# Ten of ten rows per gather and float32r scores in a talking-heads attention followed by two feed-forward stages

## The chip, the cores and the metric

One NeuronCore of a Trainium2 chip runs the whole program. The metric is the device time of one execution in microseconds. TensorE (PE in the profile; PEld is its weight load) multiplies, VectorE (DVE), ScalarE (ACT) and GpSimd (POOL) do the element-wise work, and SyncE's queue (SPq) issues the data transfers.

## The reference, cut to what matters

There are 4 batches, 12 heads, 448 positions and a head width of 64. Scores are mixed across the heads before the softmax (`w_pre`) and the probabilities are mixed across the heads after it (`w_post`). Two feed-forward stages on 1792 tokens of width 768 follow.

```python
scores = scale * np.matmul(q, k.transpose(0, 1, 3, 2))
scores = np.einsum('bhij,hg->bgij', scores, w_pre)
attn = softmax(scores)                       # over the last axis
attn = np.einsum('bhij,hg->bgij', attn, w_post)
x = (attn @ v), heads side by side           # 1792 x 768
h = x @ w_in;  x = (h * clip(h + 3, 0, 6) / 6) @ w_out     # 768 -> 2048 -> 768
return ((x @ w1) * (x @ w2)) @ w3 @ w_out2   # 768 -> 1024 -> 1024 -> 768
```

The feed-forward weights arrive as 64-bit floats; the kernel unpacks them itself. q, k and v are float32.

## The kernel before

**Attention.** The 448 query rows of a batch are cut into four chunks (`ci`, 16 in all). For a chunk, `load_q` (line 344) loads q, and for every first chunk of a batch `load_k` (line 353) loads k in three pieces. `scores` (line 366) is called six times per chunk, each time for two heads, 96 times in all: one head has its 64 contraction rows in partitions 0 to 63, the other in 64 to 127. Each is one float32 matmul of 64 rows by 110 or 120 query columns against 448 keys, into a PSUM bank of its own. The trace shows a float32 matmul as two instructions, so a call has four. `out` (line 387) copies the two heads to the tile `s`, whose partitions are queries, by ScalarE or VectorE.

**The mix.** `mix` (line 392) handles one slot: two groups of nine query rows of one batch. There are 25 slots per batch, 100 in all. Each group is fetched by `gather` (line 403), a transfer that turns ten partitions of `s` (nine query rows of this group and one that belongs to another) times twelve heads into 120 partitions of the tile `g`: rows 0 to 59 carry five query rows with their twelve heads, rows 60 to 119 the other five. `premix` (line 411) multiplies by block weights in four quarters of the array (4 matmuls, 8 instructions), `rowmax` (line 419, VectorE) takes the maximum, `softexp` (line 424, ScalarE, two halves) the exponentials and their sums, `guard` (line 431, GpSimd as a rule) adds 1e-9, `recip` and `weigh` (lines 436 and 441, VectorE) make weights of the reciprocal, and `postmix` (line 455) multiplies by them in 32 small float32 matmuls (64 instructions). `evac` (line 469) copies the result out of PSUM in two parts. After the slots of half a batch, `values` (line 479) multiplies by v, six calls per half batch, 48 in all, and the result goes to DRAM through the tile `x`.

**Feed-forward.** Line 598 on: `Line.weight` loads each block of weights, unpacks it on ScalarE and VectorE, and splits it into a high and a low float32r part; `product` (line 679) then makes three float32r products (high x high, high x low, low x high). `up` (line 688) and `down` (line 708) are its users.

**The order of the work** is written by a planner before the program starts. `Plan.add` (line 99) takes the engine or the choice of engines, an estimated duration and a priority; `Plan.run` (line 135) plays the program through with those estimates and fixes for each engine the order in which it runs its instructions. On the chip each engine follows that order, and an instruction that waits holds up everything behind it on its engine. `URGE` (line 69) holds offsets of the priorities and the slot pace, `unit0`, 3.845. For work that can go to several engines the first named is preferred; another takes it if the preferred one is planned busy for more than a set number of nanoseconds (`pGuard`, 226.69, for the guard). `SHARED` (line 72) says which tiles live in which buffers; `BUFS` (line 262) how many there are: 4 of `g`, 5 of `k`, 3 of `q`, 4 of `x`, and 4 pairs of PSUM banks shared by all matmuls. The first feed-forward weights may start to load when the last q load (`gate["q"]`, line 349) has been issued and landed.

The lines that later steps rest on:

```python
GROUP = 9
GROUPS = [12, 12, 13, 13]
BLOCKS = G0[4] // 2
...
mm(p.t[:M, i, :S], q.t[d, hp * M:(hp + 1) * M], k.t[d, hp % 2], True, True)
op = plan.add("PE", 950, prio, emit, read=(q, k), ...
...
nc.sync.dma_start(out=g.t[:120, y], in_=st.t[p0:p0 + 9 * d + 1:d])
...
plan.add({"Pool": 250, "DVE": 140}, 0, at + URGE["norm"], guard, use=(z,), wait="Guard")
```

## Time and profile before

| what | value |
|---|---|
| three runs, us | 1309.34, 1313.62, 1320.05 (median 1313.62) |
| profiled execution: span from first to last instruction, us | 1319.0 |
| profiled execution: own time | no other figure than the span is listed; of the three runs the highest, 1320.05, lies nearest, 1.05 above it |
| TensorE busy | 1270.9 us, 96% |
| VectorE busy | 924.2 us, 70% |
| ScalarE busy | 490.4 us, 37% |
| GpSimd busy | 344.8 us, 26% |
| mean granted TensorE clock | 0.991 |

A busy time is the sum of an engine's instructions, not a share of its peak. Instructions of TensorE overlap, so the step from the start of one operation to the start of the next tells more than the duration of one. The line number of every matmul is 237, that of the helper which issues it; the tile names (`sc`, `pre`, `post`, `val`, `up`, `dn`) tell them apart.

### The profile page before, as it was taken

Reading aid. Unit: us, or ns where it says so; the run is one execution under the profiler, and the core shown is the slowest. Engines: PE = TensorE matmul, PEld = TensorE weight load, DVE = VectorE, ACT = ScalarE, POOL = GpSimd, SP = SyncE. Lnnn points to the kernel's source line nnn. Section 1 sums busy time; section 2 is a strip of 40 time slices with the busy share of each in tenths; the row PEclk is TensorE's granted clock in tenths of the full one; section 3 lists DMA queues with packets and bytes.
Section 4 is the critical chain, followed back from the end, with each engine's and each line's share of the span. In section 5 each row is a group of like instructions: output and inputs, shape, how many; then the busy total and the mean of one; then the engine's idle time right before and its main releaser. Section 6 shows DMA issues by size and latency. Waiting matters only on the chain.

```text
span 1319.0 us, 30151 instructions
## 1 busy us (share of the span) xinstructions
PE 1270.9 (96%) x12768; PEld 1033.1 (78%) x12768; DVE 924.2 (70%) x1424; ACT 490.4 (37%) x972; POOL 344.8 (26%) x311
## 2 busy tenths in 40 slices
PE   7899999999989999999999999999999999999998
PEld 3446555555568899889898989998989999999997
DVE  2667766757697789989989988966357556654533
ACT  5656655556575442232322232333134111111110
POOL 0000000000034344443234333334443222322211
PEclk9999999999999999999999999999999999999999
DMA  5766746646664334323232233314443111211003
GB/s 150 205 180 157 239 144 173 209 131 177 190 210 140 132 108 135 116 86 93 91 96 88 88 112 104 95 52 139 151 144 100 37 39 46 60 37 36 12 28 140
DMA packets 75574, 154.06 MB, mean 117 GB/s; under 512 B 7152, under 2 KB 42672, under 8 KB 75440
## 3 DMA queue, kind: packets, MB, share of 16 engines
q1 hardware_dynamic: 75440, 152.14, 38.2%
q8 instruction: 100, 1.64, 0.5%
q14 instruction: 34, 0.28, 0.1%
HBM read 88.32 MB, written 20.78 MB: 83 GB/s over the span
## 4 chain that ended last, share of the span: by engine, by line
PE 44%; DVE 12%; DMA 4%; issue 3%; POOL 1%; ACT 1%; POOLq 0%; SPq 0%; DVEq 0%
PE up L237 24%; PE dn L237 16%; PE w L237 5%; DVE raw L637 2%; DMA raw<-w_in 2%; DVE raw L641 2%; DVE raw L639 2%; DVE raw L633 1%; DVE acc L729 1%; DVE raw L631 1%; DVE w L644 1%; DMA w3dram<-raw 1%; ACT raw L624 1%; POOL raw L644 1%; DMA raw<-w_out 1%
## 5 line engine op out<-in xcount | busy, mean ns | idle before, releaser
L237 PE MATMUL up<-act,w 128*128 128x448 f32 x2160 | 458.9, 366 | 0.0
L237 PEld LDWEIGHTS up<-act,w 128*128 128x128 f32 x2160 | 404.7, 188 | 37.1
L237 PE MATMUL dn<-gs,w 128*128 128x448 f32 x1728 | 376.2, 369 | 10.4 <-POOL gs L240 7.3
L237 PEld LDWEIGHTS dn<-gs,w 128*128 128x128 f32 x1728 | 324.6, 189 | 44.4 <-POOL gs L240 10.8
L729 DVE TENSOR_TENSOR acc<-acc,dn 128x896 f32<-128x896 f32 x168 | 181.4, 1081 | 79.1 <-PE dn L237 77.5
L240 POOL TENSOR_TENSOR w<-raw,w 128x768 fp32r<-128x768 f32 (+1 forms) x65 | 126.8, 1952 | 206.7 <-ACT w L312 129.0
L240 POOL TENSOR_TENSOR gs<-t,gs 128x448 fp32r<-128x448 f32 (+1 forms) x58 | 95.2, 1642 | 300.8 <-ACT gs L312 290.9
L237 PEld LDWEIGHTS post<-wt,e 60*64 60x64 f32 (+1 forms) x6400 | 111.4, 137 | 63.3 <-issue 42.7
L624 ACT ACTIVATE raw<-raw 128x384 f32<-128x384 f32 (+1 forms) x136 | 71.5, 528 | 234.5 <-DMA raw<-w 68.2
L427 ACT ACTIVATE e<-pre,m 128x448 f32<-128x448 f32 x200 | 125.9, 637 | 36.9 <-DVE m L421 30.4
L421 DVE TENSOR_REDUCE m<-pre 128x2 f32<-128x896 f32 x100 | 107.6, 1086 | 42.4 <-PE pre L237 41.7
L237 PE MATMUL post<-wt,e 60*64 60x60 f32 (+1 forms) x6400 | 118.5, 222 | 17.2 <-issue 12.6
L312 ACT CAST gs<-t 128x448 fp32r<-128x448 f32 (+1 forms) x60 | 45.0, 750 | 192.1 <-DVE t L885 124.4
L432 POOL TENSOR_SCALAR z<-z 128x2 f32<-128x2 f32 x97 | 21.9, 226 | 353.3 <-ACT e L427 349.9
L237 PE MATMUL pre<-g,wih 56*64 56x448 f32 (+1 forms) x800 | 104.8, 561 | 8.6 <-DMA g<-s 6.8
L237 PE MATMUL sc<-k,q 64*120 64x448 f32 (+1 forms) x384 | 93.6, 588 | 5.0 <-DMA k<-kd 5.0
L631 DVE TENSOR_SCALAR raw<-raw 128x768 f32<-128x768 f32 (+1 forms) x68 | 61.6, 907 | 42.8 <-ACT raw L624 39.6
L637 DVE SCALAR_TENSOR_TENSOR raw<-raw 128x384 int32<-128x384 int32 (+1 forms) x136 | 79.5, 623 | 1.6
L641 DVE SCALAR_TENSOR_TENSOR raw<-raw 128x384 f32<-128x384 uint32 (+1 forms) x136 | 79.2, 608 | 0.3
L312 ACT CAST w<-raw 128x768 fp32r<-128x768 f32 (+1 forms) x55 | 43.6, 793 | 79.8 <-PE w L237 30.2
L237 PE MATMUL w<-w 128*128 128x512 f32 (+1 forms) x384 | 68.6, 337 | 0.0
L237 PEld LDWEIGHTS pre<-g,wih 60*64 60x64 f32 (+1 forms) x800 | 24.9, 133 | 55.7 <-issue 15.7
(69 smaller groups left out, 1114.6 us busy)
## 6 DMA issues: line engine op xcount, KB each, us to landing
g<-s SPq DMA_DIRECT2D x200, 210.0 KB
raw<-w SPq DMA_DIRECT2D x48, 384.0 KB
raw<-w_in SPq DMA_DIRECT2D x28, 384.0 KB
raw<-w_out SPq DMA_DIRECT2D x28, 384.0 KB
raw<-w3t SPq DMA_DIRECT2D x32, 256.0 KB
v<-vd SPq DMA_DIRECT2D x12, 512.0 KB
raw<-w4dram SPq DMA_DIRECT2D x16, 384.0 KB
k<-kd SPq DMA_DIRECT2D x12, 448.0 KB
```

Of the source, the lines that this page charges most:

```text
L237: nc.tensor.matmul(o, lhsT=lt, rhs=rh, start=start, stop=stop)
L240: eng.tensor_tensor(out=o, in0=a, in1=b, op=ALU.subtract)
L312: nc.scalar.copy(o, i)
L421: nc.vector.tensor_reduce(out=m.t, in_=pre.t[:, :, :S], axis=AX.X, op=ALU.max, negate=True)
L427: nc.scalar.activation(out=e.t[:, a_], in_=pre.t[:, a_, :S], func=ACTF.Exp, bias=m.t[:, a_:a_ + 1], accum_out=z.t[:, a_:a_ + 1])
L624: nc.scalar.mul(value()[:, halves[i]], f(bits(i))[:, :, 1], 2.0 ** -112)
L631: one(out=f(y), in0=f(y), scalar1=F64_TOP, scalar2=-F64_TOP, op0=ALU.min, op1=ALU.max)
L637: two(out=y, in0=hi, scalar=-0x80000000, in1=y, op0=ALU.bitwise_and, op1=ALU.bitwise_or)
L639: one(out=hi, in0=y, scalar1=-0x800000, scalar2=None, op0=ALU.bitwise_and)
L641: two(out=f(hi), in0=lo, scalar=2.0 ** -52, in1=f(hi), op0=ALU.mult, op1=ALU.mult)
L644: (nc.gpsimd if e == "Pool" else nc.vector).tensor_tensor(out=o[:, halves[i]], in0=x[:, halves[i]], in1=f(bits(i))[:, :, 1], op=ALU.add)
L729: nc.vector.tensor_tensor(out=o(), in0=o(), in1=p.t[:, :, :S], op=ALU.add)
```

## The change

A group is now ten query rows, all ten that a gather fetches, and a slot is twenty: 23 slots per batch, the last of which holds one group (8 of whose ten rows exist), 92 slots and 180 gathers in all (200 before). The gather lands at partitions 4 to 123 of `g`, so that the two sets of five rows lie in partitions 4 to 63 and 64 to 123; partitions 0 to 3 are set to zero by a new GpSimd memset (`blank`) that each slot's gathers wait for. Chunks become 120, 120, 110 and 98 query rows.

The scores become three float32r products per head (high x high, high x low, low x high), six matmuls per call in place of two float32 ones. For them a new function `halve` splits each load of q and of k into a high and a low part: q in two pieces (six for the first chunk), k in two. The high part is a copy, on GpSimd, or on ScalarE or VectorE if GpSimd is planned busy for over 123 ns; the low part is a subtraction, on GpSimd or VectorE. Raw loads of both share the three `q` buffers, the k halves have six `k` buffers, the q halves four new `u` buffers; `w` goes from 5 to 1 (with `u` added to its places) and `x` from 4 to 2. The scratch space of dynamic transfers is set to 1024, and offsets in `URGE` change with the pace left at 3.845.

```diff
 
 SET = 5
 ROWS = 12 * SET
-GROUP = 9
-GROUPS = [12, 12, 13, 13]
-APART = [g - 1 for g in GROUPS]
+GROUP = 2 * SET
+BEFORE = 64 - ROWS
+GROUPS = [12, 12, 11, 10]
 G0 = [sum(GROUPS[:c]) for c in range(5)]
-BLOCKS = G0[4] // 2
...
 LEN = [GROUP * g for g in GROUPS[:3]]
 LEN.append(S - sum(LEN))
-WIDE = [10 * d for d in APART]
+WIDE = [GROUP * d for d in GROUPS]
...
-            first, d = group_rows(c, t)
-            G = G0[c] + t
-            for i, r in enumerate((0, 1, 2, 3, 4, 6, 7, 8, 9)[:GROUP - (G >= G0[4] - 2)]):
-                order[WD0[c] + first + d * r] = GROUP * G - (G == G0[4] - 1) + i
+            for r in range(GROUP):
+                row = GROUP * (G0[c] + t) + r
+                if row < S:
+                    order[WD0[c] + t + GROUPS[c] * r] = row
...
 SHARED = dict(
-    accs=("pth",), acts=("ptl",), gs=("e", "g"), t=("e", "g"), act0=("s",), act3=("s",),
-    w=("k", "w"), raw=("q", "raw"), early=("w0", "w1", "w2", "k"), first=("q", "r0", "r1", "r2", "raw"), stg=("x",), stage=("raw", "w"),
+    accs=("pth",), acts=("ptl",), kraw=("q",), qraw=("q",), khl=("k",), qhl=("u",), gs=("e", "g"), t=("e", "g"), act0=("s",), act3=("s",),
+    w=("k", "u", "w"), raw=("q", "raw"), early=("w0", "w1", "w2", "k", "u"), first=("q", "r0", "r1", "r2", "raw"), stg=("x",), stage=("raw", "w"),
...
     BUFS = {
-        "s": (kp, [120, H, S], F32, 2), "k": (kp, [128, 2, S], F32, 5), "q": (kp, [128, DM], F32, 3),
+        "s": (kp, [120, H, S], F32, 2), "k": (kp, [128, 2, S], F32, 6), "q": (kp, [128, 2, S], F32, 3), "u": (kp, [128, DM], F32, 4),
+        "kraw": (kp, [128, 2, S], F32, 0), "qraw": (kp, [128, DM], F32, 0), "khl": (kp, [128, 2, S], F32R, 0), "qhl": (kp, [128, DM], F32R, 0),
         "e": (kp, [128, 2, S], F32, 4), "g": (kp, [128, 2, S], F32, 4), "gs": (kp, [128, 2, S], F32R, 0), "t": (kp, [128, 2, S], F32, 0),
         "act0": (kp, [128, 2, KC, S], F32R, 0), "act3": (kp, [128, 2, KC, S], F32R, 0),
-        "w": (None, [128, DM], F32R, 5), "raw": (None, [128, DM], I32, 3),
+        "w": (None, [128, DM], F32R, 1), "raw": (None, [128, DM], I32, 3),
...
         "pth": (pth, [128, JC * H, UMAX], F32, 1), "ptl": (ptl, [128, JC * H, UMAX], F32, 1),
-        "v": (vp, [128, 4, JC, D], F32, 3), "x": (vp, [128, 2, UMAX], F32, 4),
+        "v": (vp, [128, 4, JC, D], F32, 3), "x": (vp, [128, 2, UMAX], F32, 2),
...
+    def halve(prio, raw, kind, pieces):
+
+        h, l = Buf(kind), Buf(kind)
+        first, parts = None, []
+        for n in pieces:
+            size = S if isinstance(n, tuple) else n.stop - n.start
+            at = n if isinstance(n, tuple) else (slice(None), n)
+
+            def high(e, at=at, first=first is None):
+                if first:
+                    take(h, l)
+                if e == "Pool":
+                    nc.gpsimd.tensor_copy(h.t[at], raw.t[at])
+                else:
+                    copy(e, h.t[at], raw.t[at])
+
+            def low(e, at=at):
+                minus(e, l.t[at], raw.t[at], f(h.t)[at])
+            op = plan.add({"Pool": 150 + size * 17 // 10, "ACT": 190 + size * 5 // 6, "DVE": 70 + size}, 0, prio + URGE["halve"], high, read=(raw,),
+                          new=() if first else (h, l), hold=(h, l), after=(first,) if first else (), wait="Half")
+            first = first or op
+            parts.append(plan.add({"Pool": 150 + size * 12 // 5, "DVE": 70 + size * 5 // 4}, 0, prio + URGE["halve"], low, after=(op,), hold=(raw, h, l), wait="Half"))
+        return h, l, parts
+
     def load_q(prio, ci):
         z = "0" if ci == 0 else ""
         b, c = divmod(ci, 4)
         n, o = 6 * WIDE[c], 6 * WD0[c]
-        q = qtile[ci] = Buf("q")
+        q = Buf("qraw")
         gate["q"] = dma_in(prio + URGE["load" + z], qd[b, :, o:o + n], q, lambda t: t[:, :n], ns=1300)
         if ci > 1:
             loads.append((gate["q"], cstart[ci - 2]))
+        pieces = 6 if ci == 0 else 2
+        qtile[ci] = halve(prio, q, "qhl", [slice(i * n // pieces, (i + 1) * n // pieces) for i in range(pieces)])
 
     def load_k(prio, b, i):
         z = "0" if b == 0 else ""
-        k = ktile[b, i] = Buf("k")
+        k = Buf("kraw")
         op = dma_in(prio + URGE["load" + z], kd[b, i], k, lambda t: t.rearrange("p a s -> p (a s)"), ns=1600)
         if b:
             loads.append((op, cstart[4 * b - 2] + 4))
+        ktile[b, i] = halve(prio, k, "khl", [(slice(None), j) for j in range(2)])
 
     def load_v(prio, b, hq):
         z = "0" if b == 0 else ""
...
-        k, q = ktile[b, hp // 2], qtile[ci]
+        (kh, kl, ks), (qh, ql, qs) = ktile[b, hp // 2], qtile[ci]
 
         def emit():
             take(p, *dest)
-            for i in range(2):
-                d = slice(i * D, (i + 1) * D)
-                mm(p.t[:M, i, :S], q.t[d, hp * M:(hp + 1) * M], k.t[d, hp % 2], True, True)
-        op = plan.add("PE", 950, prio, emit, read=(q, k), new=(p, *dest), hold=(st,), after=() if dest else (st.first,))
+            for n, (x, y) in enumerate(((qh, kh), (qh, kl), (ql, kh))):
+                for i in range(2):
+                    d = slice(i * D, (i + 1) * D)
+                    mm(p.t[:M, i, :S], x.t[d, hp * M:(hp + 1) * M], y.t[d, hp % 2], n == 0, n == 2)
+        op = plan.add("PE", 660, prio, emit, new=(p, *dest), hold=(st, qh, ql, kh, kl), after=(ks[hp % 2], qs[hp * len(qs) // 6], *(() if dest else (st.first,))))
...
-        for y in range(2):
+        both = range(min(2, G0[4] - 2 * t))
+        used = slice(0, PIECE * len(both))
+
+        def blank():
+            take(g)
+            nc.gpsimd.memset(g.t[:BEFORE], 0.0)
+        blanked = plan.add("Pool", 900, at + URGE["gather"] - 1, blank, new=(g,))
+        for y in both:
             G = 2 * t + y
             c = next(c for c in range(4) if G < G0[c + 1])
-            p0, d = group_rows(c, G - G0[c])
+            p0, d = G - G0[c], GROUPS[c]
             st = stile[4 * b + c]
 
             def gather(y=y, st=st, p0=p0, d=d):
-                if y == 0:
-                    take(g)
-                nc.sync.dma_start(out=g.t[:120, y], in_=st.t[p0:p0 + 9 * d + 1:d])
-            op = gathers[s, y] = plan.add("SP", 1250, at + URGE["gather"], gather, read=(st,), new=() if y else (g,), hold=(g,), chain=("g", s), issue=760)
-            if y:
-                g.writers.append(op)
+                nc.sync.dma_start(out=g.t[BEFORE:BEFORE + 2 * ROWS, y], in_=st.t[p0:p0 + 9 * d + 1:d])
+            gathers[s, y] = plan.add("SP", 1250, at + URGE["gather"], gather, read=(st,), after=(blanked,), hold=(g,), chain=("g", s), issue=760)
+            g.writers.append(gathers[s, y])
 
         def premix():
             take(pre, e)
-            for y in range(2):
+            for y in both:
...
                 for a_ in range(2):
-                    i, o = slice(PIECE * a_, 120 if a_ else ROWS), slice(PIECE * y, PIECE * (y + 1))
+                    i, o = slice(PIECE * a_, PIECE if a_ == 0 else PIECE + ROWS), slice(PIECE * y, PIECE * (y + 1))
...
-                    for y in range(2):
-                        i, o = slice(PIECE * y, PIECE * y + ROWS - 12 * a_), slice(k % 2 * PIECE, (k % 2 + 1) * PIECE)
+                    for y in both:
+                        i, o = slice(PIECE * y, PIECE * y + ROWS), slice(k % 2 * PIECE, (k % 2 + 1) * PIECE)
                         c0 = 256 * a_ + k // 2 * ROWS
                         mm(post.t[o, y, c0:c0 + ROWS], e.t[i, a_, k0:k0 + PIECE], w.t[i, a_], True, True)
...
-    own = np.where(p < ROWS, p // H, np.where((p < 72) | (p >= 120), -1, (p - 72) // H))
+    own = np.where((p < BEFORE) | (p >= BEFORE + 2 * ROWS), -1, (p - BEFORE) // H % SET)
     own2 = np.where(p % PIECE < ROWS, p % PIECE // H, -1)
     consts = np.concatenate([
-        w_pre[p % H], w_post[p % PIECE % H],
+        w_pre[(p - BEFORE) % H], w_post[p % PIECE % H],
         *((x[:, None] == np.arange(SET)[None]).astype(np.float32) for x in (own, own2)),
     ], axis=1)
```

## Rows read from the trace of the kernel before

**Rows 1.** The page: busy time per engine, and the chain that ended last.

```profile
PE 1270.9 (96%) x12768; PEld 1033.1 (78%) x12768; DVE 924.2 (70%) x1424; ACT 490.4 (37%) x972; POOL 344.8 (26%) x311
PE 44%; DVE 12%; DMA 4%; issue 3%; POOL 1%; ACT 1%; POOLq 0%; SPq 0%; DVEq 0%
```

**Rows 2.** Busy time in stretches: us, then each engine, PEclk, DMA share, GB/s.

```profile
0.00:40.00 40.00, 28.73 (x364) 13.51 (x364) 11.35 (x24) 20.82 (x39) 1.26 (x9) 1.00 0.54 150
40.00:200.00 160.00, 152.98 (x3552) 88.66 (x3552) 111.86 (x198) 97.86 (x243) 9.44 (x44) 0.98 0.64 186
200.00:360.00 160.00, 151.73 (x3494) 88.83 (x3496) 110.15 (x196) 94.42 (x230) 8.80 (x41) 0.98 0.61 175
360.00:400.00 40.00, 35.40 (x823) 25.09 (x820) 34.89 (x69) 28.55 (x72) 14.90 (x16) 0.96 0.62 190
440.00:720.00 280.00, 271.21 (x1321) 248.40 (x1320) 251.38 (x379) 87.60 (x131) 108.12 (x71) 0.99 0.33 102
```

**Rows 3.** Timeline of TensorE in a steady stretch: start, us, what.

```profile
199.85 1.01 PE L237 MATMUL sc<-k,q 64*110 64x448 f32 x4
200.78 0.98 PE L237 MATMUL pre<-g,wih 60*64 60x448 f32 x8
201.59 1.11 PE L237 MATMUL post<-wt,e 60*64 60x60 f32 x64
202.63 1.01 PE L237 MATMUL sc<-k,q 64*110 64x448 f32 x4
203.56 0.98 PE L237 MATMUL pre<-g,wih 60*64 60x448 f32 x8
204.48 1.01 PE L237 MATMUL sc<-k,q 64*110 64x448 f32 x4
205.41 1.16 PE L237 MATMUL post<-wt,e 60*64 60x60 f32 x64
206.50 1.01 PE L237 MATMUL sc<-k,q 64*110 64x448 f32 x4
```

**Rows 4.** Timeline at the start: score weight loads, first copies, first gathers.

```profile
5.04 11.56 PE L237 MATMUL sc<-k,q 64*110 64x448 f32 x48 [5.04 <-DMA k<-kd]
12.29 0.19 PEld L237 LDWEIGHTS sc<-k,q 64*110 64x110 f32 x2 [0.19 <-issue]
12.66 0.19 PEld L237 LDWEIGHTS sc<-k,q 64*110 64x110 f32 x2 [0.19 <-issue]
13.22 13.44 SPq L406 DMA_DIRECT2D g<-s  x10
```

**Rows 5.** The chain in order of time: start, us, what; float32r products of feed-forward.

```profile
1292.33 3.73 PE up L237 x18
```

**Rows 6.** Timeline of TensorE at the end of attention: the values calls.

```profile
402.96 9.62 PE L237 MATMUL val<-ptl,v 128*64 128x232 f32 x96 [1.05 <-ACT ptl L312]
```

**Rows 7.** Groups with shapes kept apart, 0 to 540 us: busy us, mean ns, idle before.

```profile
L240 POOL TENSOR_TENSOR act<-stg,act 128x448 fp32r<-128x448 f32 x5 | 6.3, 1255 | 6.0 <-ACT act L312 5.8
L240 POOL TENSOR_TENSOR gs<-t,gs 128x896 fp32r<-128x896 f32 x8 | 17.5, 2185 | 15.2 <-ACT gs L312 15.2
L432 POOL TENSOR_SCALAR z<-z 128x2 f32<-128x2 f32 x97 | 21.9, 226 | 353.3 <-ACT e L427 349.9 <-DVE m L421 3.2
L943 POOL MEMSET const-float32-0.0<- 128x1 f32 x1 | 0.1, 99 | 0.2 <-issue 0.2
L312 ACT CAST act<-stage 128x448 fp32r<-128x448 f32 x12 | 6.3, 569 | 0.9 <-DMA stage<-xdram 0.8
L240 DVE TENSOR_TENSOR act<-stage,act 128x448 fp32r<-128x448 f32 x6 | 3.8, 665 | 2.0 <-ACT act L312 2.0
```

**Rows 8.** Instructions of the tile wt: ns min/median/max, first and last start.

```profile
L443 DVE TENSOR_TENSOR wt<-wip,r x100: 267/282/1825, 24.2 to 397.5; 128x120 f32<-128x120 f32 x100
```

**Rows 9.** Waits 40 to 360 us: who waited for whom, total us, times, longest.

```profile
PEld post L237 <- issue: 40.4, 84, 3.8
PE post L237 <- issue: 12.6, 8, 3.6
PEld post L237 <- ACT e L427: 7.0, 11, 0.7
PEld pre L237 <- DMA g<-s: 2.9, 3, 1.1
PE post L237 <- DVE wt L443: 1.7, 1, 1.7
```

**Rows 10.** SyncE's queue, whole span: its waits, total us, times, longest.

```profile
SPq L406 <- PE pre L237: 50.2, 39, 3.9
```

**Rows 11.** Timeline of SyncE's queue, 296 to 320 us: start, us, what.

```profile
296.51 1.38 SPq L325 DMA_DIRECT2D q<-qd  x1
298.00 1.43 SPq L516 DMA_DIRECT2D xdram<-x  x1
299.52 17.26 SPq L406 DMA_DIRECT2D g<-s  x12
```

More of the change, by code (lines that the diff above doesn't have):

```diff
@@ L60, in query_order @@
         for t in range(GROUPS[c]):
[L61 to L64 removed]
+            for r in range(GROUP):
+                row = GROUP * (G0[c] + t) + r
+                if row < S:
+                    order[WD0[c] + t + GROUPS[c] * r] = row
     return order
[L69 removed]
+URGE = dict(pPool=8.169, pACT=9869.74, pDVE=108010.89, pOut=1.06, pHalf=123.479, halve=0.0, pGuard=226.69, pCopy=4.98, pRest=91.937, pEvac=114.434, load0=37.1, load=-4.77, gather=-159.49, pre=-12.85, max=-15.206, exp=32.931, norm=20.31, post=2.04, evac=44.28, values=11.36, step=14.3, vload=17.524, vload0=-26.4, lead=-24.47, begin=-9.6, consts=-75.04, moe=53.91, rows=83.36, win=-45.468, wout=-28.65, w34=-25.69, w2=27.34, unit0=3.845, unit1=8.407, unit2=10.44, w34us=64.443)
 SHARED = dict(
[L73 to L74 removed]
+    accs=("pth",), acts=("ptl",), kraw=("q",), qraw=("q",), khl=("k",), qhl=("u",), gs=("e", "g"), t=("e", "g"), act0=("s",), act3=("s",),
+    w=("k", "u", "w"), raw=("q", "raw"), early=("w0", "w1", "w2", "k", "u"), first=("q", "r0", "r1", "r2", "raw"), stg=("x",), stage=("raw", "w"),
     sc=("pp",), pre=("pp",), post=("pp",), val=("pp",), up=("pp",), dn=("pp",), w34=("pp",))
@@ L420, in rowmax @@
             take(m)
-            nc.vector.tensor_reduce(out=m.t, in_=pre.t[:, :, :S], axis=AX.X, op=ALU.max, negate=True)
+            nc.vector.tensor_reduce(out=m.t[used], in_=pre.t[used, :, :S], axis=AX.X, op=ALU.max, negate=True)
         plan.add("DVE", 1080, at + URGE["max"], rowmax, use=(pre,), new=(m,))
@@ L426, in softexp @@
                 take(z)
-            nc.scalar.activation(out=e.t[:, a_], in_=pre.t[:, a_, :S], func=ACTF.Exp, bias=m.t[:, a_:a_ + 1], accum_out=z.t[:, a_:a_ + 1])
+            nc.scalar.activation(out=e.t[used, a_], in_=pre.t[used, a_, :S], func=ACTF.Exp, bias=m.t[used, a_:a_ + 1], accum_out=z.t[used, a_:a_ + 1])
         for a_ in range(2):
@@ L432, in guard @@
             (nc.gpsimd if eng == "Pool" else nc.vector).tensor_scalar(
-                out=z.t, in0=z.t, scalar1=1e-9, scalar2=None, op0=ALU.add)
+                out=z.t[used], in0=z.t[used], scalar1=1e-9, scalar2=None, op0=ALU.add)
         plan.add({"Pool": 250, "DVE": 140}, 0, at + URGE["norm"], guard, use=(z,), wait="Guard")
@@ L469, in evac @@
         def evac(eng, a_):
[L470 to L473 removed]
+            ny = len(both)
+            size = min(GROUP, S - 2 * GROUP * t)
+            n = min(SET, size - SET * a_)
+            o = pt.t[:, :, c0:c0 + ny * size].rearrange("p c (y i) -> p y c i", y=ny)[:, :, :, SET * a_:SET * a_ + n]
+            i = post.t[:, :ny, 256 * a_:256 * a_ + JC * ROWS].rearrange("p y (c i) -> p y c i", i=SET)[:, :, :, :n]
             copy(eng, o, i)
```

17 lines of the change are left out of this document (5 added, 12 removed).

## The prediction

> **What bounds the kernel now.** I read the page's shares first, then the chain, then stretches, then single operations. TensorE is busy for 1270.9 of 1319 us, and the chain that ended last is mostly its work [rows 1]; that chain starts only in the feed-forward part, so attention has to be read by stretches. Between 40 and 360 us TensorE is busy for 152.98 + 151.73 of 320 us, which is 95%, while VectorE stands at 69%, ScalarE at 60% and GpSimd at 6% [rows 2]. Attention is therefore bound by TensorE, with little idle time to win: 15.3 us in that stretch and 11.3 us in the first 40 us, where it waits for the first gathers. What TensorE waited for in the stretch is mostly "issue", nothing that the profile shows; the softmax chain cost it 7.0 + 1.7 us and the gathers 2.9 us [rows 9]. From 440 to 720 us it is busy for 271.21 of 280 us, and there VectorE stands at 251.38, 90% [rows 2]. So time that TensorE saves in attention should bring everything behind it forward, unless VectorE stops that.
>
> The **price of an operation** is the step from its start to the next one's start. The score calls take 0.93 us each (199.85 to 200.78, 202.63 to 203.56, 204.48 to 205.41), the premix 0.81 and 0.92, mean 0.87, the postmix 1.04 and 1.09, mean 1.07 [rows 3]. Six values calls take 9.62 us, 1.60 each [rows 6]. As a check: 96 x 0.93 + 100 x 1.94 + 48 x 1.60 = 89 + 194 + 77 = 360 us, against the 369 us of TensorE busy before 400 us (the sum of the first four stretches), where some feed-forward products run already.
>
> **The change part by part.**
>
> *Eight slots fewer.* The slots go from 100 to 92, and each costs TensorE 0.87 + 1.07 = 1.94 us: -15.5 us. The last slot of a batch holds one group, and I give nothing for that: its matmuls run in two quarters of the array, not four, and as many after each other as before. The postmix contracts 60 rows where its second half had 48, with the columns that set its time unchanged.
>
> *Scores.* The two halves overlap now: on the way in, one score call follows another in 0.74 us, two instruction pairs of 0.37 us (12.29 to 12.66), each with 0.19 us of weight loads and 0.19 us of idle time between them [rows 4]. In the mixed stretch a call takes 0.93, so entering from another shape costs 0.19. The new call has three pairs. No row shows a float32r product in row halves; the nearest is the feed-forward one over 128 rows and the same 448 columns, 3.73 / 18 = 0.207 us [rows 5]. If the halves go on overlapping, a call takes 3 x 0.207 + 0.19 = 0.81; with 0.19 a pair, where its weight loads set a floor, 0.76. I take 0.78: 96 x 0.15 = 14.4 us less. The far ends are a call without the entry, 3 x 0.19 = 0.57 (-35 us), and one whose halves follow each other, 6 x 0.207 + 0.19 = 1.43 (+48 us).
>
> *Splits.* There are 12 k loads in 2 pieces of 448 columns and 16 q loads, 15 in 2 pieces of 300 to 360 and the first in 6 of 120. The nearest GpSimd row is a subtraction over 448 columns at 1.26 us [rows 7], the upper end for a copy too. If GpSimd takes all of it: 24 x 2 x 1.26 = 60 us for k, and 30 x 2 x 0.96 + 6 x 2 x 0.34 = 62 for q. The memset lies between 0.10 us for one column and 2.19 us for a two-input operation over its 896 [rows 7]; I take 1.0, nearer to half of the latter since it reads nothing: 92 us. With 92 guards of 0.226 (21 us) GpSimd has about 235 us of work in some 370, 63%; what goes to ScalarE (0.57 a piece) or VectorE (0.67) [rows 7] finds 40% and 31% free. This work is not on TensorE's path as long as the pieces are ready a call ahead, and loads go out long before: price 0. If that cover is gone, the second rival below gives the cost.
>
> *At the start* nothing covers it. The first score starts at 5.04 us when its load lands [rows 4]; now a ScalarE copy (0.57) and a subtraction (0.67 on VectorE, 1.26 on GpSimd) come before it [rows 7], +1.2 to +1.8 us, and the pieces behind share ScalarE and VectorE with the score copies. Three pairs cost less than four instructions there. +2 us, ends 0 and +5.
>
> *Blank before the gathers.* Each slot's first gather now waits for a memset, which waits for the tile to come free. Behind the memset on GpSimd stand guards and splits, behind the gather on SyncE's queue the q, k and v loads and the stores of x [rows 11]. The gathers already stood 50.2 us in 39 waits for the premix that frees `g` [rows 10], and yet TensorE missed them for only 2.9 us [rows 9]: four tiles give each gather about 4 x 3.9 us (some 390 us over 100 slots). One more us disappears in that, 0; were it exposed on those 39, it would be 39. Twenty gathers fewer, 20 x 17.26 / 12 = 29 us of that queue [rows 11], speak for the 0.
>
> *Waits behind GpSimd.* A guard that arrives while GpSimd is busy waits: 0.63 x half of 1.0 us = 0.3. The weights `wt` behind it, two SBUF inputs on VectorE, take 0.282 as a rule, but 1.825 at the most [rows 8], where GpSimd's long subtractions have begun. Splits fill about 122 of 370 us, so 0.33 x 0.6 = 0.2 on average. 0.5 x 92 = 46 us of delay in the softmax chain, from 0 to 46 on TensorE. The chain has been delayed little for TensorE so far, 8.7 us in 320 [rows 9], so I take a tenth: +5.
>
> *At no cost.* Two evacuation copies widen from 384 to 480 columns on engines with 30 to 40% free. Two `x` tiles in place of four: a result leaves in one store, issued in 1.43 us [rows 11], with three results per half batch of 45 us; uncovered, the third would wait, 8 x 1.43 = 11 us. Values move as many columns as before. The weight tiles of feed-forward go from 10 to 11.
>
> *Sum.* Idle time shrinks with the slots by 8% of 27: -2. In all -15.5 - 14.4 + 2 + 5 - 2 = -25 us. Against the profiled span of 1319.0 that is 1294; the median of the runs lies 5.4 under that span, so the same step from 1313.6 gives **1288**.
>
> **The rivals.**
>
> *More is won.* The entry costs less with one-pass products, a call takes 0.66, and no wait appears: -15.5 - 26 - 2 = -43.5, **1270**. For it: the 0.19 of entry is a difference of two rows, not an operation of its own. Chance 0.08.
>
> *GpSimd's delay reaches TensorE by half.* -15.5 - 14.4 + 2 - 2 + 23 = -7, **1307**. For it: orders are fixed from estimates, and TensorE stands wherever one `wt` is late. Against: 8.7 us so far. Chance 0.14.
>
> *VectorE holds the feed-forward.* Attention leaves VectorE 31% free, and 28 us less of attention takes some 9 us of that from the weights unpacked toward its end; at 90% busy afterwards it would hand them to TensorE: +9, **1297**. Chance 0.07.
>
> *Slower: GpSimd's queue stands at a split whose load is late.* Every guard and blank queued behind it stands too, and with them softmax and gathers. The longest wait of SyncE's queue for `g` was 3.9 us [rows 10], with loads queued behind it. 25 loads after the first ones x 3.9 = 98 us, half of it on TensorE 49: -30 + 49 + 0 = +19, **1333**. It decides from (13 + 30) / 25 = 1.7 us per load. Against: GpSimd's guard can go to VectorE, and the q buffers, freed after a split and not after six score calls, let loads go out earlier. Chance 0.09.
>
> *Slower: score rounds don't overlap with their weight loads.* Each pair then takes 0.19 + 0.19, a call 3 x 0.38 + 0.19 = 1.33, 96 x 0.40 = +38: -15.5 + 38 + 5 = +28, **1341**; with halves in turn 1351. Against: in [rows 4] 0.37 a pair with 0.19 of loads is matmul time throughout, the loads hidden, and the feed-forward's 0.207 hides them too. The Trainium skill (TensorE: Matmul & The Clock Gate, "The mechanism") has weight loads overlap running matmuls only when their row groups differ; here the next round uses the same two, and by that the sum would be the +28 of this rival. The 0.37 of this trace disagrees with it, for float32 at least. Chance 0.06.
>
> **How the numbers follow.** The forecast has the remaining 0.56, with 1280 to 1302 as its own range (a call of 0.76 to 0.81, a start 0 to 5 us later, waits of 0 to 12). About 1%, 13 us, is what a measurement of this kernel tells from no change. Faster: 0.56 + 0.08 + 0.07 = 0.71. Within 1%: 0.14. Slower: 0.09 + 0.06 = 0.15. Leaving out both slower cases and a little of the third and the first rival, 1270 to 1310 holds 8 in 10.
>
> **What would show it.** Right: a TensorE timeline with score calls of 0.76 to 0.81 us and six instructions, 92 slots with premix and postmix as before, the values of the last half batch about 25 us before 402.96, and 440 to 720 us alike when shifted. Wrong: score calls over 0.93 us; TensorE waits for `wt` or `e` of over 20 us in attention; GpSimd waiting for q or k loads with guards behind; TensorE clearly less busy in the feed-forward than 97%.

## The result, and the profile after

The changed kernel takes **1299.47 us** (median of 17 runs, 1290.43 to 1309.74), the kernel before, run beside it, 1316.57 (17 runs): a ratio of **0.989, 95% interval 0.9862 to 0.9918**, which is 14.5 us less (11 to 18) where the forecast had 25 less. (The ratios are estimated from the single runs and are not quotients of the medians, which here would be 0.987.) In a later series the same pair gave 0.9961 (0.9929 to 0.9993, e9 below), some 5 us less. So the gain is real and small: in the first series it lies between the forecast's -25 and the -7 of the rival in which GpSimd's delay reaches TensorE by half, in the later one it is about that rival's. The profiled execution of the changed kernel took 1303.46 us, with a span of 1301.7.

The page of the changed kernel, busy time per engine and the chain that ended last, answers to [rows 1]:

```profile
PE 1241.3 (95%) x12240; PEld 1038.5 (80%) x12240; DVE 940.6 (72%) x1433; ACT 490.0 (38%) x950; POOL 482.4 (37%) x456
PE 66%; DVE 16%; issue 7%; DMA 6%; ACT 3%; POOL 2%; SPq 0%; POOLq 0%; DVEq 0%; ACTq 0%
...
L425 POOL MEMSET g<- 4x896 f32 x92 | 76.1, 837 | 104.4 <-PE pre L231 94.2
```

TensorE does 29.6 us less (1270.9 before). The span shrank by 17.3 in these two profiles: some 12 us of the work saved came back as idle time. GpSimd works 138 us more; the last row, from the page's list of the costliest groups, is the memset, 0.837 us each where 1.0 was taken.

The steady stretch of TensorE after, its timeline (start, us, what), answers to [rows 3], and the last values call to [rows 6]:

```profile
208.99 1.11 PE L231 MATMUL post<-wt,e 60*64 60x60 f32 x64
210.03 0.87 PE L231 MATMUL sc<-khl,qhl 64*110 64x448 f32 x6
210.82 0.98 PE L231 MATMUL pre<-g,wih 64*64 64x448 f32 x8
211.99 1.16 PE L231 MATMUL post<-wt,e 60*64 60x60 f32 x64 [0.18 <-ACT pth L307]
213.07 0.87 PE L231 MATMUL sc<-khl,qhl 64*110 64x448 f32 x6
...
373.48 8.66 PE L231 MATMUL val<-ptl,v 128*64 128x208 f32 x96
```

A score call with three pairs lasts from 210.03 to 210.82, 0.79 us (forecast 0.78, before 0.93), and the postmix 1.04 and 1.08, as before. The last values end at 373.48 + 8.66 = 382.1; before they ended at 402.96 + 9.62 = 412.6. Attention ended 30 us earlier here, and from there to the end it now takes 1301.7 - 382.1 = 919.6 us, where it took 906.4. Part of these 13 us is no loss. Before its last values call began, the kernel before had already run 36 `up` products on its first feed-forward weights, the changed kernel 9 (groups of TensorE, first of before from 0 to 402.9 us, then of after from 0 to 373.4):

```profile
L237 PE MATMUL up<-act,early 128*128 128x448 f32 x36 | 8.9, 384 | 0.0
```

```profile
L231 PE MATMUL up<-act,early 128*128 128x448 f32 x9 | 2.1, 377 | 0.0
```

At 0.207 us each, 27 products are 5.6 us of feed-forward work that moved from the stretch of attention to behind it. So attention itself became some 25 us shorter, as forecast, and some 7.6 us were given back behind it.

Busy time in stretches after (us, each engine, PEclk, DMA share, GB/s) answers to [rows 2]; the last three rows are the seam behind the last values, the steady feed-forward, and the stretch used for all kernels below:

```profile
0.00:40.00 40.00, 29.57 (x482) 17.79 (x484) 26.50 (x45) 24.50 (x51) 21.19 (x36) 1.00 0.61 203
40.00:200.00 160.00, 145.28 (x3396) 93.84 (x3394) 119.82 (x211) 105.21 (x244) 65.84 (x105) 0.97 0.55 173
200.00:360.00 160.00, 146.78 (x3530) 96.22 (x3528) 125.59 (x226) 108.54 (x256) 65.86 (x104) 0.98 0.59 181
...
382.00:462.00 80.00, 69.52 (x323) 60.76 (x321) 61.75 (x83) 35.68 (x57) 40.34 (x29) 0.98 0.47 143
440.00:720.00 280.00, 273.12 (x1328) 249.73 (x1328) 245.52 (x368) 79.63 (x121) 113.87 (x73) 0.99 0.33 100
40.00:330.00 290.00, 268.22 (x6290) 174.35 (x6286) 221.41 (x391) 192.30 (x447) 118.90 (x190) 0.98 0.57 176
```

Between 40 and 360 us TensorE is busy for 292 of 320 us, 91% instead of 95%: 27.9 us idle where [rows 2] had 15.3. GpSimd went from 18.2 us of work in that stretch to 131.7. The same views of the kernel before, for the seam and the common stretch:

```profile
40.00:330.00 290.00, 275.26 (x6310) 159.39 (x6312) 200.61 (x358) 175.71 (x432) 16.74 (x78) 0.98 0.63 180
...
412.50:492.50 80.00, 77.53 (x373) 70.80 (x372) 62.59 (x92) 40.76 (x61) 35.04 (x22) 0.98 0.47 149
```

In the 80 us after the last values TensorE lacks 10.5 us after the change and 2.5 before. The steady feed-forward, 440 to 720 us, is as it was (273.12 and 271.21 busy), so nothing there shows VectorE holding it back more than before.

The waits of the changed kernel between 40 and 360 us (who waited for whom: total us, times, longest) answer to [rows 9]:

```profile
POOL g L425 <- PE pre L231: 83.9, 46, 6.3
POOL z L459 <- ACT e L454: 66.2, 40, 5.9
...
PE post L231 <- issue: 9.9, 6, 3.3
PE pre L231 <- issue: 4.0, 7, 1.7
...
POOL khl L351 <- DMA kraw<-kd: 7.6, 3, 2.9
...
POOL qhl L351 <- DMA qraw<-qd: 6.3, 5, 2.8
...
PE post L231 <- DVE wt L470: 2.6, 2, 1.6
PE post L231 <- DVE z L459: 2.4, 2, 2.1
```

GpSimd now stands in two places that were not there before: at the memset until the premix frees `g`, and at splits whose load has not landed (13.9 us in 8 waits). TensorE's waits for `wt` and `z` are small when read by name. Half of its idle time, 13.9 of 27.9 us, is called "issue", for which the profile shows no cause (before, 12.6 of 15.3 [rows 9]), so what the waits cost cannot be read from this list; the experiments price them.

### The profile page after: what moved, and what is told of

Read it like the earlier page. It is cut to its first block, busy times and chain, and to the rows that moved or that the text cites. A ratio compares the mean times of both kernels' runs of the same rounds, so it can differ in the third digit from the quotient of the medians.

```text
span 1301.7 us, 29318 instructions
## 1 busy us (share of the span) xinstructions
PE 1241.3 (95%) x12240; PEld 1038.5 (80%) x12240; DVE 940.6 (72%) x1433; ACT 490.0 (38%) x950; POOL 482.4 (37%) x456
## 4 chain that ended last, share of the span: by engine, by line
PE 66%; DVE 16%; issue 7%; DMA 6%; ACT 3%; POOL 2%; SPq 0%; POOLq 0%; DVEq 0%; ACTq 0%
PE up L231 26%; PE dn L231 18%; PE post L231 6%; PE w L231 5%; PE pre L231 4%; PE val L231 4%; PE sc L231 3%; DVE raw L665 2%; DVE raw L661 2%; DMA raw<-w_in 2%; DVE raw L659 2%; DVE raw L669 1%; DVE acc L757 1%; DVE raw L667 1%; ACT e L454 1%
## 5 line engine op out<-in xcount | busy, mean ns | idle before, releaser
L234 POOL TENSOR_TENSOR w<-raw,w 128x768 fp32r<-128x768 f32 (+1 forms) x63 | 122.2, 1940 | 177.5 <-ACT w L307 95.2
L231 PEld LDWEIGHTS post<-wt,e 60*64 60x64 f32 x5760 | 98.9, 138 | 49.5 <-issue 28.3
L454 ACT ACTIVATE e<-pre,m 128x448 f32<-128x448 f32 (+1 forms) x184 | 116.0, 636 | 34.6 <-DVE m L448 27.6
L231 PE MATMUL post<-wt,e 60*64 60x60 f32 x5760 | 106.6, 224 | 20.8 <-issue 11.8
L425 POOL MEMSET g<- 4x896 f32 x92 | 76.1, 837 | 104.4 <-PE pre L231 94.2
L448 DVE TENSOR_REDUCE m<-pre 128x2 f32<-128x896 f32 (+1 forms) x92 | 98.6, 1085 | 19.1 <-PE pre L231 18.3
L231 PE MATMUL pre<-g,wih 64*64 64x448 f32 (+1 forms) x720 | 94.8, 566 | 5.7 <-issue 4.0
L231 PE MATMUL sc<-khl,qhl 64*120 64x448 f32 (+2 forms) x576 | 78.3, 395 | 12.1 <-ACT khl L307 5.8
L231 PEld LDWEIGHTS sc<-khl,qhl 64*120 64x120 f32 (+2 forms) x576 | 46.9, 179 | 46.8 <-issue 7.0
L672 POOL TENSOR_TENSOR raw<-raw 128x256 f32<-128x256 f32 (+1 forms) x37 | 44.4, 1203 | 68.1 <-DVE raw L669 58.0
```

What stands on the lines that cost most here:

```text
L231: nc.tensor.matmul(o, lhsT=lt, rhs=rh, start=start, stop=stop)
L234: eng.tensor_tensor(out=o, in0=a, in1=b, op=ALU.subtract)
L425: nc.gpsimd.memset(g.t[:BEFORE], 0.0)
L448: nc.vector.tensor_reduce(out=m.t[used], in_=pre.t[used, :, :S], axis=AX.X, op=ALU.max, negate=True)
L454: nc.scalar.activation(out=e.t[used, a_], in_=pre.t[used, a_, :S], func=ACTF.Exp, bias=m.t[used, a_:a_ + 1], accum_out=z.t[used, a_:a_ + 1])
L672: (nc.gpsimd if e == "Pool" else nc.vector).tensor_tensor(out=o[:, halves[i]], in0=x[:, halves[i]], in1=f(bits(i))[:, :, 1], op=ALU.add)
```

## The experiments

Kernels e1 to e4, e5 to e8 and e9 to e12 each ran on one chip with runs of the kernel before, with medians of 1305.63, 1309.38 and 1306.71 us. All ratios are to these. The changed kernel itself ran in the first series and as e9, but not beside e1 to e8.

**The two parts alone.** e1 has the ten rows and the memset and keeps the changed kernel's priorities, with scores, loads and buffers as before:

```
- (kh, kl, ks), (qh, ql, qs) = ktile[b, hp // 2], qtile[ci]
+ k, q = ktile[b, hp // 2], qtile[ci]
...
+ mm(p.t[:M, i, :S], q.t[d, hp * M:(hp + 1) * M], k.t[d, hp % 2], True, True)
```

> The changed kernel with its ten-row groups and blanks, but the scores as two float32 products again: no splits, buffers of k, q, w and x as before. Theory (TensorE's work in attention sets the gain, and each part gives its share): attention is about 15 us shorter than before, of which about half arrives at the end, so 1303 to 1310 where before has 1316 (ratio 0.991 to 0.996). Rival (the splits on GpSimd eat what the scores save, the rows give nearly all): ratio 0.985 to 0.990, as the changed kernel's 0.989 or better.

It took 1283.31 us, 0.9831 (0.9778 to 0.9885): 22 us less than before (15 to 29), and by value more than the whole change gives. That is below both expected ranges, on the side of the rival. Whether the changed priorities have a share in it was not run.

e2 has the scores and splits alone, with the nine rows and 100 slots of before, and the buffers and priorities of after:

```
+ for n, (x, y) in enumerate(((qh, kh), (qh, kl), (ql, kh))):
...
- lead=-24.47
+ lead=-21.47
```

> The kernel before with its nine-row groups and 100 slots, but float32r scores and the splits (priorities and buffers of the changed kernel, one priority offset moved by 3 so that the planner finds an order). Theory: score calls of 0.76 us, attention about 15 us shorter, about half of it at the end: ratio 0.991 to 0.996. Rival (splits eat it): ratio 0.997 to 1.004, with more waits of TensorE for the softmax chain.

It took 1325.05 us, 1.013 (1.008 to 1.0179): 17 us more, although each score call is cheaper, and above both expected ranges. This part loses, here with two `x` tiles and with priorities that were chosen for ten rows, which may have a share in the loss. Its profiled execution was its longest, with a span of 1339.9 us, so its rows of GpSimd's waits between 40 and 330 us tell where it stood, not how much that costs:

```profile
POOL z L461 <- ACT e L456: 159.6, 50, 8.6
POOL qhl L357 <- DMA qraw<-qd: 19.4, 4, 6.2
```

Four q splits stood at their loads, for up to 6.2 us, in the queue that also carries the guards.

**Does VectorE hold the feed-forward?** e3 is the kernel before and e4 the changed one, both with VectorE's unpacking of the weights cut to 32 columns:

```
- y = m.t[:, :n]
+ y = m.t[:, :32]
...
- y, hi, lo = m.t[:, halves[i]], bits(i)[:, :, 1], bits(i).bitcast(U32)[:, :, 0]
+ y, hi, lo = m.t[:, halves[i]][:, :32], bits(i)[:, :32, 1], bits(i).bitcast(U32)[:, :32, 0]
```

> The kernel before, same order on every engine, with the five VectorE operations that unpack each block of feed-forward weights cut to 32 columns (the weights come out wrong). The comparison for the next run. TensorE idle time in the feed-forward should shrink from about 13 us between 412 and 712 us by most of that: ratio 0.988 to 0.994.

> The same cut in the changed kernel. Theory (VectorE's unpacking at the seam between attention and feed-forward took back some 12 us of what attention saved): the changed kernel gains more from the cut than the one before, and the step between the two cut kernels grows from 14 to 17 us to 24 to 28: ratio to before 0.968 to 0.974. Rival (the seam's loss lies in the rows' path through DRAM, the two x buffers and the gathers' queue, and not in VectorE): the step between the two cut kernels stays 14 to 17 us, ratio about 0.977 to 0.982.

e3 gave 0.997 (0.9934 to 1.0006), e4 0.9851 (0.9808 to 0.9894). The step between them is 0.012 x 1305.6 = 16 us, about that between the uncut kernels of the first series (14.5), and the step that the rival had. Against the 5 us of the later series it would be a growth, so the times alone do not settle it. (e3 also missed its own range, 0.988 to 0.994: relieving VectorE gave the kernel before 0.3%, not separated from nothing.) The two profiles help: behind the last values e3 takes 1309.1 - 410.9 = 898.2 us and e4 1288.6 - 380.3 = 908.3, still 10 apart where the uncut pair is 13 apart. So VectorE's unpacking is not what kept most of the gain from the end. e4's stretches show the relief (VectorE is the third engine):

```profile
440.00:720.00 280.00, 280.00 (x1358) 254.26 (x1357) 185.35 (x390) 80.72 (x123) 105.06 (x72) 1.00 0.32 100
```

VectorE fell from 245.52 to 185.35 us and TensorE filled the stretch; the ratio moved by 0.4% from the first series, within the two intervals.

**One wait taken away at a time.** e5 tells the planner that later q and k loads land 4.5 us later, so that it places the splits behind them; e6 takes all split work off GpSimd; e7 keeps four `g` tiles zeroed once, without the 92 memsets:

```
+ hop = self.HOP[op["eng"]] + op.get("late", 0)
...
+ gate["q"]["late"] = 4500
...
+ op["late"] = 4500
```

```
- op = plan.add({"Pool": 150 + size * 17 // 10, "ACT": 190 + size * 5 // 6, "DVE": 70 + size}, 0, ...
+ op = plan.add({"ACT": 190 + size * 5 // 6, "DVE": 70 + size}, 0, ...
- parts.append(plan.add({"Pool": 150 + size * 12 // 5, "DVE": 70 + size * 5 // 4}, 0, ...
+ parts.append(plan.add({"DVE": 70 + size * 5 // 4}, 0, ...
```

```
+ late = {"gt": vp.tile([128, 4, 2, S], F32, name="gt")}
+ nc.gpsimd.memset(late["gt"][:BEFORE], 0.0)
...
- blanked = plan.add("Pool", 900, at + URGE["gather"] - 1, blank, new=(g,))
```

> The changed kernel, but the planner counts each later q and k load as landing 4.5 us later, so that their splits stand later in the order of ScalarE, VectorE and GpSimd. Theory (these engines stand at splits whose load has not landed, 23 us in all between 40 and 330 us, with guards, maxima and exponentials queued behind): those waits nearly vanish, TensorE is busy for 272 to 276 us of 40 to 330 us where the changed kernel has 268, ratio to before 0.980 to 0.985. Rival (the standing at loads hides in slack; the splits' own work is what delays): ratio 0.987 to 0.991 as for the changed kernel.

> The changed kernel with no split work on GpSimd: high parts on ScalarE or VectorE, low parts on VectorE alone. Theory of the lock (VectorE's two-input operations and splits stretch, up to 3.4 us, because GpSimd's splits run beside them): VectorE's splits keep to 0.63 us, TensorE is busy for over 272 of 290 us, ratio 0.980 to 0.986. Rival (VectorE's time is what is short, 75% busy with in-order waits): some 35 us more work on VectorE delays maxima and copies, ratio 0.990 to 1.000.

> The changed kernel with four g tiles kept through attention and their partitions 0 to 3 set to zero once, so that no slot has a memset on GpSimd; from the end of attention their place in feed-forward is taken by four other tiles. Theory (GpSimd stands 81 us at memsets that wait for the premix, with guards and splits behind): TensorE's waits for the weights and the guard in attention shrink, ratio 0.982 to 0.986. Rival (guards wait for nothing that matters): ratio 0.987 to 0.991.

e5 0.9896 (0.9829 to 0.9964), e6 0.9927 (0.9892 to 0.9962), e7 0.9924 (0.9885 to 0.9963). The changed kernel itself had 0.989 and 0.9961 in its two series. All three lie between these, e5 and e6 in their rival's range and e7 just above it. As the changed kernel did not run on this chip, these runs cannot tell an effect of about 1% from none, for any of the three causes. The profiles say somewhat more. In e6 VectorE's subtractions of k no longer stretch (0.626 us at the most) and TensorE is busy for 272.6 of 290 us, both as the theory had it, yet the ratio is the rival's. In e5 no split waits for a load between 40 and 360 us any more, and the last values end at 371.5 us where the changed kernel has 382.1.

**The rows with kept tiles.** e8 is e1 with e7's kept `g` tiles:

> The ten-row kernel with float32 scores (0.983), also with g kept and without memsets. Theory: GpSimd has the guards alone, as before the change; ratio 0.978 to 0.982. Rival: the same 0.983, within its interval.

It took 1276.87 us, **0.9792 (0.9732 to 0.9852)**. That is the fastest of all kernels here, and its interval lies wholly below both of the changed kernel's, though these are from other series. It lies in the range that the theory had, but from e1's it is not separated, so what the memset costs is not shown. Ten rows alone beat the whole change, on one chip with e11 against e9 below.

**The whole change again, and the split work alone.** e9 is the changed kernel unaltered, a control on the chip of the last four. e10 is the same without the split work behind the start: all chunks use the first q pieces and all batches the first k pieces, while all loads still go out and the products are as many. With the split work go the waits of the later score calls for a load, and the planner writes another order:

```
+ if ci:
+     qtile[ci] = qtile[0][0], qtile[0][1], qtile[0][2][::3]
+     return
...
+ if b:
+     ktile[b, i] = ktile[0, i]
+     return
```

> The changed kernel once more, unaltered, beside the next three on one chip: ratio 0.989 as before, within 0.985 to 0.992.

> The changed kernel without the split work after the start: every chunk uses the halves of the first q load, every batch those of the first k loads; the other loads still go out and nobody reads them (the scores are wrong). The six matmuls of a score call stay. Theory (split work on ScalarE, VectorE and GpSimd, which runs ahead of the softmax chain in their fixed orders, takes back what the cheaper score calls save): attention ends 8 to 12 us earlier, TensorE busy for over 276 of 290 us from 40 to 330, ratio 0.980 to 0.984. Rival (the splits hide; the fixed order built on a too low price of a score call, 660 ns, or the four PSUM pairs hold TensorE): TensorE busy for 266 to 271 us as in the changed kernel, ratio 0.987 to 0.991.

e9 took 1302.68 us, 0.9961 (0.9929 to 0.9993), outside the range expected from the first series, and e10 1292.0 us, 0.9869 (0.982 to 0.9917). The intervals don't meet: the split work, with its waits and in the order that it brings, costs 0.0092 x 1306.7 = **12 us** on one chip. e10's time is at the edge of the rival's range, while its last values end at 371.8 us, 11.8 before e9's, as the theory had it. The stretch from 40 to 330 us, first of e9, then of e10 (TensorE is the first engine, GpSimd the fifth):

```profile
40.00:330.00 290.00, 262.71 (x6265) 171.29 (x6268) 217.52 (x387) 189.84 (x442) 115.40 (x189) 0.98 0.56 174
```

```profile
40.00:330.00 290.00, 274.12 (x6674) 178.49 (x6666) 212.83 (x378) 192.13 (x451) 86.66 (x159) 0.99 0.61 187
```

With 29 us of GpSimd's work gone, TensorE's idle time in that stretch falls from 27.3 to 15.9 us, and it issues 409 more matmuls. e10's profiled execution was its fastest, with a span 21 us below e9's, so these differences are larger than those of the medians.

**Tiles of x, and the planner's price.** e11 is e1 with two `x` tiles, as the change has them; e12 is the changed kernel whose planner counts a score call at 780 ns:

```
- "x": (vp, [128, 2, UMAX], F32, 4),
+ "x": (vp, [128, 2, UMAX], F32, 2),
```

```
- op = plan.add("PE", 660, prio, emit, ...
+ op = plan.add("PE", 780, prio, emit, ...
```

> The ten-row kernel with float32 scores (0.983), but with two x tiles in place of four, as in the changed kernel; nothing else moves. Theory (the two x tiles, which also stage the rows that the feed-forward reads back, cost the seam): the feed-forward from the last values call to the end grows by 5 to 10 us, ratio 0.987 to 0.991. Rival (the seam lost time for other reasons): ratio 0.981 to 0.985.

> The changed kernel with the planner's price of a score call set from 660 to 780 ns, what the trace shows; only the orders change. Theory of the price: attention ends 5 to 10 us earlier and the ratio falls to 0.981 to 0.985. Rival: the orders adapt little, ratio 0.986 to 0.993.

e11 took 1288.99 us, 0.9869 (0.9821 to 0.9916), between the two expected ranges, against 0.9831 for e1 on another chip: not separated, so whether fewer `x` tiles cost some 4 us stays open. The profiles point that way: behind the last values e11 takes 909.1 us and e1 1279.5 - 374.9 = 904.6. e12 gave 0.9902 (0.9865 to 0.9939), the rival's range. Its interval overlaps e9's by 0.001, so a gain of (0.9961 - 0.9902) x 1306.7 = 8 us from the right price is likely and not shown. Its last values end at 373.0 us, 10.6 before e9's, with all split work still there, though in its second shortest execution of twelve. So the order that the planner writes for the splits can move the end of attention about as far as taking them away does (371.8).

e11 serves for more: it is the changed kernel without scores and splits, and with the buffers that these need set back, on e9's chip. Its stretch:

```profile
40.00:330.00 290.00, 278.73 (x6280) 161.54 (x6274) 207.07 (x357) 183.63 (x437) 80.87 (x155) 0.98 0.57 180
```

TensorE is idle for 11.3 us of it, less than in e10 (15.9) and e9 (27.3).

## Why the prediction was right, and where its sizes failed

**Direction and range held, in part by luck:** the kernel is faster, by 1.1% where the forecast had 1.9%. The two halves of the sum came out on opposite sides of zero: the rows won what was forecast or more, the scores with their splits lost where a gain was forecast. In the later series that left 5 us of the 25, the size of the rival at -7; that the first series came out nearer to the forecast is nothing that the prediction had worked out. Part by part:

*Eight slots fewer, with idle time:* forecast -15.5 - 2 = -17.5. e11 measured -17 (-11 to -23), e1 -22 (-15 to -29), memset and changed priorities and all. This term held.

*The price of a score call:* forecast 0.78, measured 0.79 and, from 213.07 to the next premix at 213.87, 0.80. Two calls in a row, in e12's timeline, take 1.40 us:

```profile
302.51 1.47 PE L231 MATMUL sc<-khl,qhl 64*110 64x448 f32 x12
303.91 1.16 PE L231 MATMUL post<-wt,e 60*64 60x60 f32 x64
```

The second adds 0.61, or 0.203 a pair, close to the 0.207 that was taken: the halves do overlap, and the entry costs 0.18. The rival of weight loads that don't overlap, at 1.33, is out. The Trainium skill (TensorE: Matmul & The Clock Gate, "The mechanism") lists that a weight load overlaps running matmuls only when its row group differs; beside that it names a background weight buffer whose loads are pulled ahead as well. Three pairs in the same two row halves in 0.79 us disagree with the first taken alone, for float32r, as 0.37 a pair did for float32; whether that buffer is what hides the loads, no run here shows.

*Start:* forecast +2. The first scores, in the timeline of the first microseconds after, answer to [rows 4]:

```profile
5.16 1.03 ACT L307 CAST khl<-kraw 128x448 fp32r<-128x448 f32 x2 [0.67 <-DMA kraw<-kd]
5.77 0.73 PE L231 MATMUL sc<-khl,qhl 64*120 64x448 f32 x2 [5.77 <-ACT khl L307]
...
19.21 0.97 PE L231 MATMUL pre<-g,wih 64*64 64x448 f32 x4 [0.91 <-DMA g<-s]
```

Before, the first premix began so:

```profile
17.59 0.97 PE L237 MATMUL pre<-g,wih 60*64 60x448 f32 x4 [0.99 <-DMA g<-s]
```

The scores began at 5.77 instead of 5.04 us, less late than the 1.2 to 1.8 us forecast, since only the high parts have to be there for the first products. The first premix came 1.6 us later, close to the +2.

**What failed is the pair "price 0" for the splits and "a tenth: +5" for the waits behind GpSimd,** and with it that the 14.4 us of cheaper scores come through. Scores and splits together were forecast at -14.4 + 2 + 5 = -7.4. Measured on one chip, e9 against e11, they cost (0.9961 - 0.9869) x 1306.7 = **+12 us**, with intervals that don't meet; alone on the rows of before (e2) +17. The step that failed was the clause that the splits are not on TensorE's path "as long as the pieces are ready a call ahead". Readiness for TensorE was not the question: the splits stand in the queues of the softmax chain. The "tenth" rested on 8.7 us of waits, of which 7.0 are those of the weight loads (PEld) and only 1.7 TensorE's own [rows 9], and it priced GpSimd's queue alone. e10 prices the split work at 12 us. Without it, the cheaper products bring nothing that shows in the times either: e10 and e11 have the same ratio, 0.9869, where 96 x 0.14 = 13 us apart was due.

Where the time went is seen in the stretches from the start to the end of the last values (TensorE is the first engine), of e9, e10 and e11 in turn:

```profile
0.00:383.60 383.60, 339.32 (x7834) 221.73 (x7834) 288.46 (x510) 248.09 (x572) 158.89 (x251) 0.99 0.57 176
```

```profile
0.00:371.80 371.80, 337.09 (x7834) 220.78 (x7834) 265.79 (x474) 238.71 (x552) 123.07 (x213) 0.98 0.59 182
```

```profile
0.00:377.00 377.00, 351.67 (x7645) 206.53 (x7646) 262.73 (x459) 235.83 (x550) 110.44 (x198) 0.97 0.56 177
```

Against e11, TensorE works 12.4 us less in e9 and 14.6 less in e10, so the cheaper scores are there (some of it may be the granted clock, which is lowest in e11: 0.99, 0.98 and 0.97). But it is idle for 44.3 us in e9 and 34.7 in e10, against 25.3 in e11. In e9 the 19.0 us of idle time more outweigh the work saved, and attention ends 6.6 us later; in e10 9.4 of the 14.6 us go that way. What idles TensorE in e10, with no split left after the start, stays open.

The forecast also put the work on the wrong engine. It gave GpSimd all of it and counted 63% busy. In the changed kernel GpSimd is 41% busy between 40 and 360 us (131.7 of 320): of some 89 us of splits it runs about 48, ScalarE about 10, and VectorE about 31. VectorE also carries the maximum, the reciprocal and the weights of each slot; it went from 69% to 77% busy in that stretch (245.4 of 320 us).

How a late split reaches TensorE can be seen once in full. The chain of the changed kernel between 246 and 260 us, in order of time (start, us, what):

```profile
246.31 8.18 DMA kraw<-kd
...
254.51 1.01 DVE khl L309
255.53 0.07 DVE r L465
255.60 1.39 DVE khl L234
257.00 0.19 DVE wt L470
257.19 0.09 DVE z L459
...
257.33 1.16 PE post L231 x64
```

And the timeline of all engines there (in brackets the idle time before, and what ended it):

```profile
248.66 0.56 POOL L351 CAST khl<-kraw 128x448 fp32r<-128x448 f32 x1 [2.42 <-DMA kraw<-kd]
...
252.38 0.56 ACT L307 CAST khl<-kraw 128x448 fp32r<-128x448 f32 x1 [2.04 <-DMA kraw<-kd]
...
253.03 3.49 POOL L234 TENSOR_TENSOR khl<-kraw,khl 128x448 fp32r<-128x448 f32 x3 [0.63 <-ACT khl L307]
...
254.51 1.01 DVE L309 CAST khl<-kraw 128x448 fp32r<-128x448 f32 x1 [2.29 <-DMA kraw<-kd]
...
256.60 0.76 POOL L459 TENSOR_SCALAR z<-z 128x2 f32<-128x2 f32 x2
...
257.33 1.16 PE L231 MATMUL post<-wt,e 60*64 60x60 f32 x64 [2.06 <-DVE z L459]
```

The k load takes 8.18 us. All three engines stand at a cast that needs one: GpSimd 2.42 us, ScalarE 2.04, VectorE 2.29. VectorE's cast then takes 1.01 us and its subtraction 1.39, both beside GpSimd's three subtractions; the weights `wt`, whose reciprocal was done at 255.60, stand behind that subtraction in VectorE's queue, and the postmix starts at 257.33, 2.06 us late. GpSimd starts its next two guards only at 256.60, after its subtractions; how long they had been ready these lines do not tell. The fourth rival had the first half of this right (a split whose load is late, with the softmax chain behind it), but not the queue: here it is VectorE's. Nor was its size met. It would have decided at 1.7 us of TensorE's time per load; GpSimd's 8 waits come to 13.9 us over 25 later loads, 0.6 each even if all of it had reached TensorE. And e5, in which no split waits for its load, was not measurably faster, though its attention ended 10.6 us earlier in the profile. So late loads are one way in which the split work costs its 12 us. How much falls to them, to the places of the splits in three queues (which e12's order, too, changes), and to the stretching told next, these runs do not tell apart.

*Stretching.* The forecast counted GpSimd's long reads at 0.2 us per `wt`. The instructions on the tiles `khl` and `wt` in the changed kernel (ns min/median/max; the last answers to [rows 8]):

```profile
L234 POOL TENSOR_TENSOR khl<-kraw,khl x14: 1123/1148/1539, 5.9 to 255.2; 128x448 fp32r<-128x448 f32 x14
...
L234 DVE TENSOR_TENSOR khl<-kraw,khl x10: 610/622/1605, 8.9 to 255.6; 128x448 fp32r<-128x448 f32 x10
...
L309 DVE CAST khl<-kraw x5: 382/395/3399, 9.5 to 254.5; 128x448 fp32r<-128x448 f32 x5
...
L470 DVE TENSOR_TENSOR wt<-wip,r x92: 266/282/1654, 24.3 to 368.7; 128x120 f32<-128x120 f32 x88, 64x120 f32<-64x120 f32 x4
```

The median `wt` is still 0.282 us. The forecast was of a mean, and that rose between 40 and 330 us from 0.279 (21.8 us over 78) to 0.312 (23.7 over 76): 0.03 and not 0.2, so this small term was too high. But VectorE's cast of 0.395 us once took 3.4, from 165.48 us on, while GpSimd ran three subtractions from 165.31 to 168.63, and its subtraction of 0.622 took up to 1.6. The Trainium skill (SBUF — State Buffer, "Who interferes with whom") has VectorE's casts (in a mode that uses both port pairs) and its operations with two SBUF inputs contend with GpSimd for a shared port pair; the 3.4 us beside GpSimd's subtractions agree with it. e6, with no split on GpSimd, was not measurably faster, so this alone is hardly the cost, though e6 also gave VectorE more to do.

*Memset before the gathers, at 0:* no run speaks against it; e7 and e8 without it are not separated from the changed kernel and e1. *VectorE holds the feed-forward:* not borne out by e3 and e4. *440 to 720 us alike:* held, yet the seam before it was not. Behind the last values e10, with no split work, takes 1280.9 - 371.8 = 909.1 us, e11 1286.1 - 377.0 = 909.1, and e9 1302.0 - 383.6 = 918.4; the feed-forward work left at that point is the same within three products. e5 and e12, with all splits, take 916.6 and 917.5. So by these single profiles the 9 us at the seam come with the split work too, though the last split starts at 307.8 us in e9 and 303.6 in the first profile. What carries them over is not shown. In the 80 us behind attention TensorE's named waits, all for the feed-forward's activations, come to 7.9 us in the changed kernel, 2.5 in the kernel before, 7.1 in e11 and 4.3 in e10, so they follow neither the splits alone nor the end of attention alone.

## What to carry to other kernels

A cheaper operation on the busiest engine can lose its whole price difference if what prepares it rides in the in-order queues that carry the dependent chain of the same loop, as it did here. Price such preparation by the waits of the whole chain behind it, not by the free share of the engines: here GpSimd's 63% busy, forecast, or 41%, measured, was the wrong number to read. Run each part of a change alone, for here one half won 17 to 22 us, the other lost 12 to 17, and the sum still looked like a gain.

## What the runs showed that was not expected

- Three float32r pairs over 64 rows in two row halves step in 0.61 us when one call follows another, where two float32 pairs take 0.74 [rows 4]; with the entry from another shape it is 0.79 against 0.93.
- A GpSimd cast of 128 x 448 to float32r takes 0.56 us at the median of `khl`, half of its subtraction at 1.148; the upper bound for a cast, 1.26, was twice too high.
- A memset of 4 partitions x 896 columns takes 0.837 us on GpSimd, although it writes only 4 partitions; one of 128 partitions x 1 column takes 0.10 [rows 7].
- The same pair of kernels had a ratio of 0.989 in one series and 0.9961 in another, with intervals that don't meet (0.9862 to 0.9918 and 0.9929 to 0.9993); so here a difference under 1% holds only between kernels that ran side by side.
